# One transfer for a segment's rows, one buffer for the sums of q and k

## The chip, the cores and the metric

The kernel runs on one core of one Trainium2 chip. The metric is the time of one execution on the device, in microseconds; of several executions the median is taken. The core has five engines that matter here: PE (TensorE: matmuls, and PEld, its weight loads), DVE (VectorE), ACT (ScalarE), POOL (GpSimd) and SP (SyncE, which here only issues transfers). Sixteen DMA engines move the data. ACT and POOL issue transfers as well.

## What is computed

Two independent blocks are added to x. The first is attention with a recurrent memory: x is cut into 64 segments of 32 rows; each segment's attention sees 8 memory rows and its own 32, and the memory for the next segment is the attention's output at the memory rows. So segment s + 1 cannot begin before segment s is through its output projection. The second block normalizes two routed rows (C = 2) and sends them through a gated feed-forward network of width 3584; it runs at the end and is not touched by the change.

```python
def _A_ref(x, mem0, Wq, Wk, Wv, Wo, seg_len):   # x normalized, D = 1024, H = 32, E = 128, M = 8, seg_len = 32
    mem = mem0
    for s in range(n_seg):                      # 64
        xs = x[:, s * seg_len:(s + 1) * seg_len, :].copy()
        h = jnp.concatenate([mem, xs], axis=1)
        q = jnp.einsum('btd,dhe->bhte', h, Wq)
        k = jnp.einsum('btd,dhe->bhte', h, Wk)
        v = jnp.einsum('btd,dhe->bhte', h, Wv)
        scores = jnp.einsum('bhqe,bhke->bhqk', q, k) * scale
        scores = jnp.where(mask[None, None], scores, -1000000000.0)
        p = _softmax(scores, axis=-1)
        o = jnp.einsum('bhqk,bhke->bhqe', p, v)
        o = jnp.einsum('bhte,hed->btd', o, Wo)
        mem = o[:, :M, :].copy()
        outs.append(o[:, M:, :])
...
    return x + _A_ref(xn, A_mem0, A_Wq, A_Wk, A_Wv, A_Wo, A_seg_len) + _B_ref(xn, B_w_r, B_w_gate, B_w_up, B_w_down)
```

## The kernel before

**Weights.** The four matrices are cut into 64 granules of 512 KB, `g` = 0 to 63: 8 for each of the six phases q0, k0, q1, k1, v0, v1 (matrix and half of the heads, `PHASES`), and 16 for the output projection (`w` = 0 to 15). 44 granules stay in SBUF; 20 are streamed in every segment through a pool of five slots (`g`, `N_SLOT`). Of these, granule 10 is put together from copies kept in PSUM and needs no transfer (`kept_piece`), granule 19 is fetched by half. SP issues a fetch (`fetch`, L317) each time a streamed granule has been used, so the fetches run up to four granules ahead of PE. In the first segment the streamed granules are also copied to a scratch in DRAM (`wsc`), from which all later ones come.

**Rows.** A segment's 32 rows by 1024 columns lie in `XN` as 128 partitions by 256: four blocks of 256 columns (`g` in the row patterns, not a granule), each 32 partitions high. In each block the first 24 partitions (`XM`) hold the segment's first 24 rows, the other 8 the memory's. The segment's last 8 rows (the left rows) of four segments are taken together, one pass for a group `G` of four segments; `j` = s mod 4 is the place in the group. So the passes `left_pass` fall on different phases: v with j = 0, q of the next group with j = 1, k with j = 2, the left rows' output with j = 3 (`WL`). Their q and k sums go out to DRAM (`ql_d`, by `store_ql`, L656) and come back per segment as `LX` (L450), which `turn_lx` transposes at place (1, 5).

**Order.** Everything is emitted by hand. Within a segment a place is (phase, granule of the phase); `hook` puts a function behind that granule's matmuls. At the end of a phase for q or k ACT copies the sum out of PSUM into `XB` (L653); at (p + 1, 3) PE turns it (`transposes`) and it becomes `QT` or `KT`. `scores` stands at (2, 6) and (4, 6), `soften` (the softmax: exponent on ACT, then sums and products on DVE into `PT2`) at (3, 0) and (5, 0), `attend` at (5, 4), (5, 6) and in the projection. `load_seg` for the next segment is issued by POOL at (2, 0), `norm_seg` uses its rows at the segment's end. The result `WO` is copied by ACT and DVE into `OB`, which is `XN` (L752, L753), stored by POOL (L755), and turned into the next segment's memory rows. With j = 3 the left rows' result is stored a segment later, `store_left` at (2, 4), from a buffer tagged vl, which the same segment's `VL` then takes at the end of phase 4.

**Buffers.** The pool `one` has one buffer for each tag; a tile waits until all uses of the tile before it under the same tag are done. Tags that matter: bE is taken by XB of q, QT, the second PT2, and with j = 2 by XBl (the left rows' sum of k, second half, which waits there for its store to `ql_d`); kt by XB of k, KT and the first half of OT; bA by LX, the first XBl with j = 2, the first PT2, one half of VM.

**Transfers and semaphores.** Each transfer signals one of eight semaphores in turn, one ring of eight for those that SP and ACT issue, one for POOL's. An issue waits until the transfer eight places before it in its ring has landed.

Of the kernel before, what the change touches and what calls it, by code (L numbers as in the profile page):

```python
# [8 lines left out]
BF16 = mybir.dt.bfloat16  # L9
# [3 lines left out]
ACTF = mybir.ActivationFunctionType  # L13
# [15 lines left out]
def kernel(  # L29
# [16 lines left out]
    nc = tc.nc  # L46
    P = 128
# [3 lines left out]
    SEG = int(A_seg_len)  # L51
# [8 lines left out]
    SCALE = float(E) ** -0.5  # L60
    XM = SEG - M
# [3 lines left out]
    x2 = A_x[0]  # L65
    out2 = out[0]
# [27 lines left out]
    one = ctx.enter_context(tc.tile_pool(name="one", bufs=1, reuse_waits="tile"))  # L94
# [34 lines left out]
    XN = const.tile([P, 256], BF16, name="XN")  # L129
# [10 lines left out]
    SPS = BS[:, 0:8 * NK].rearrange("p (i a k) -> p i a k", i=4, a=2)  # L140
# [33 lines left out]
    for s in range(4):  # L174
        nc.vector.tensor_copy(out=SELM[:, s, :, 0:XM],
                              in_=IDENT[:, 32 * s:32 * s + XM].unsqueeze(1).to_broadcast([P, 4, XM]))
        nc.vector.tensor_copy(out=SELL[:, s, :, :],
                              in_=IDENT.rearrange("p (s c) -> p s c", c=32)[:, :, XM:SEG])
# [67 lines left out]
        return t  # L246

    def load_seg(s):
        for g in range(4):
            nc.gpsimd.dma_start(out=XN[32 * g:32 * g + XM, :], in_=x2[s * SEG:s * SEG + XM, 256 * g:256 * (g + 1)])  # L250

    def norm_seg(s):
        mr = two_rows(MR[:, s, :], "ri")
# [238 lines left out]
    for s in range(NSEG):  # L492
        G, j = divmod(s, 4)
# [7 lines left out]
        def hook(p, kc, fn):  # L501
            hooks.setdefault((p, kc), []).append(fn)
# [16 lines left out]
        def scores(half):  # L519
            QKL = qkl[0]  # L520
            q, k = QT[half], KT[half]
            for il in range(4):
                for jq in range(4):
                    hh = 4 * il + jq
                    nc.tensor.matmul(SPS[32 * jq:32 * jq + 32, il, 0, :], lhsT=q[:, hh, :], rhs=k[:, hh, :],
                                     start=(il == 0), stop=True, tile_position=(0, 32 * jq), skip_group_check=True)
                    nc.tensor.matmul(SPS[32 * jq:32 * jq + XL, il, 1, :], lhsT=QKL[:, il, 2 * half, jq, :],  # L527
                                     rhs=k[:, hh, :], start=False, stop=True, tile_position=(0, 32 * jq),
                                     skip_group_check=True)
            for S4, m in ((SPS[:, :, 0, 0:XM], MASK), (SPS[:, :, 0, SEG:NK], None),  # L530
                          (SPS[:, :, 1, SEG:NK], MASK[:, 0:XL])):
                if m is not None:
                    m = m.unsqueeze(1).to_broadcast([P, 4, S4.shape[2]])
                    nc.vector.tensor_tensor(out=S4, in0=S4, in1=m, op=ALU.add)  # L534
                else:
                    nc.vector.tensor_scalar(out=S4, in0=S4, scalar1=NEGR, scalar2=None, op0=ALU.add)
            S8 = SPS.rearrange("p i a k -> p (i a) k")
            NM = one.tile([P, 8], F32, tag="nm", name="NM")
            nc.vector.tensor_reduce(out=NM[:, :], in_=S8, axis=AX.X, op=ALU.max, negate=True)  # L539
            nc.vector.tensor_tensor(out=S8, in0=S8, in1=NM[:, :].unsqueeze(2).to_broadcast([P, 8, NK]), op=ALU.add)  # L540

        def soften(half):
            S8 = SPS.rearrange("p i a k -> p (i a) k")
            nc.scalar.activation(out=S8, in_=S8, func=ACTF.Exp, scale=SCALE)  # L544
            DN = one.tile([P, 8], F32, tag="nm", name="DN")
            nc.vector.tensor_reduce(out=DN[:, :], in_=S8, axis=AX.X, op=ALU.add)
            nc.vector.reciprocal(out=DN[:, :], in_=DN[:, :])
            PT2 = one.tile([P, 2, 4, 64], BF16, tag=("bA", "bE")[half], name="PT2")
            PTm, PTl = PT2[:, 0], PT2[:, 1]
            PM = PTl.rearrange("p i q -> p (i q)").rearrange("p (b k) -> p b k", b=8)  # L550
            PLt = PL.rearrange("p i a k -> p (i a) k")
            dnb = DN[:, :].unsqueeze(2)
            nc.vector.tensor_tensor(out=PM, in0=S8[:, :, 0:32], in1=dnb.to_broadcast([P, 8, 32]), op=ALU.mult)
            nc.vector.tensor_tensor(out=PLt[:, :, XL * j:XL * (j + 1)], in0=S8[:, :, 32:NK],
                                    in1=dnb.to_broadcast([P, 8, XL]), op=ALU.mult)
            nc.vector.transpose(out=PTm.rearrange("p i q -> p (i q)"), in_=PM.rearrange("p b k -> p (b k)"))
            nc.vector.transpose(out=PTl.rearrange("p i q -> p (i q)"), in_=PLt.rearrange("p b k -> p (b k)"))
            PTs[half] = (PTm, PTl)
# [45 lines left out]
            hook(1, 2, lambda: kept_piece(KEPT_PART, 3, nc.vector.tensor_copy))  # L604
            hook(1, 5, turn_lx)
        hook(2, 6, lambda: scores(0))
        hook(3, 0, lambda: soften(0))
        if s + 1 < NSEG:
            hook(2, 0, lambda: load_seg(s + 1))
        if j == 3 or (j == 0 and G + 1 < NT):  # L610
            hook(2 if j else 3, 0, get_left)
            hook(5, 3, prep_left)
        hook(4, 6, lambda: scores(1))
        hook(5, 0, lambda: soften(1))
        hook(5, 4, lambda: attend(0, 0))
        hook(5, 6, lambda: attend(0, 1))
# [7 lines left out]
        for p, (mat, half) in enumerate(PHASES):  # L624
            PSm = psA.tile([P, 512], F32, tag="acc", name="PSm")
            PSl, done = None, []
            if mat in left:
                PSl, done = started.pop((s, p), (None, []))
                if PSl is None:
                    PSl = psL.tile([P, 512], F32, tag="accl", name="PSl")  # L630
            rest = [8 * p + kc for kc in range(KC) if 8 * p + kc not in done]
            behind = []
            for kc in range(KC):
                g = 8 * p + kc
                Gv = granule(g)
                for jq in range(4):
                    nc.tensor.matmul(PSm[32 * jq:32 * jq + 32, :], lhsT=ST[:, kc, :], rhs=part(Gv, jq),  # L637
                                     start=(kc == 0), stop=(kc == KC - 1), tile_position=(0, 32 * jq))
                if g in KEPT_COLS and s == 0:
                    keep(g, Gv)  # L640
                behind.append((g, Gv))
                if PSl is None or kc >= 3 or not left_before:
                    for g_, Gv_ in behind:
                        if PSl is not None and g_ not in done:
                            left_pass(PSl, g_, Gv_, not done and g_ == rest[0], g_ == rest[-1])
                        after(s, g_)
                    behind = []
                for fn in hooks.pop((p, kc), []):
                    fn()
            left_before = PSl is not None  # L650
            if mat < 2:
                XB = one.tile([P, 512], BF16, tag=("bE", "kt")[mat], name="XB")
                nc.scalar.copy(out=XB[:, :], in_=PSm[:, :])  # L653
                hooks.setdefault((p + 1, 3), []).insert(0, lambda m=mat, h=half, b=XB: transposes(m, h, b))

                def store_ql(mat=mat, half=half, PSl=PSl):  # L656
                    if mat == 0:
                        XBl = left_out()[:, 2:4].rearrange("p s r h -> p (s r h)")
                    else:
                        XBl = one.tile([P, 512], BF16, tag=("bA", "vl" if s == 0 else "bE")[half], name="XBl")[:, :]  # L660
                    nc.scalar.copy(out=XBl, in_=PSl[:, :])
                    if s == 0:
                        hooks[p + 1, 3].insert(0, lambda m=mat, h=half, b=XBl: turn_first(m, h, b))
                    nc.scalar.dma_start(out=ql_d[left[mat]][2 * half + mat], in_=XBl)


                if PSl is not None and s == 0:
                    store_ql()
                elif PSl is not None and mat == 1 and half == 1:
                    nxt["ql"] = store_ql  # L670
                elif PSl is not None:
                    hooks.setdefault((p + 1, 0), []).append(store_ql)
            else:
                c0 = half * 512
                VM[half] = one.tile([P, 512], BF16, tag=("bC", "bA")[half], name="VM")
                nc.scalar.copy(out=VM[half][:, :], in_=PSm[:, :])  # L676
                if PSl is not None:
                    if half == 0:
                        group["vl"] = one.tile([P, 1024], BF16, tag="vl", name="VL")
                    nc.scalar.copy(out=group["vl"][:, c0:c0 + 512], in_=PSl[:, :])  # L680
# [70 lines left out]
        OB = XN  # L751
        nc.scalar.copy(out=OB[:, 0:P], in_=WO[:, 0:P])  # L752
        nc.vector.tensor_copy(out=OB[:, P:256], in_=WO[:, P:256])  # L753
        for g in range(4):
            nc.gpsimd.dma_start(out=out2[s * SEG:s * SEG + XM, 256 * g:256 * (g + 1)], in_=OB[32 * g:32 * g + XM, :])  # L755
        n1 = (len(fill) + 1) // 2
        for fn in fill[:n1]:
            fn()
# [119 lines left out]
```

## Time and profile before

| | us |
|---|---|
| three runs | 2021.12, 2021.41, 2036.9 |
| median | 2021.41 |
| the profiled execution | 2031.99 |
| its span, first to last instruction | 2030.4 |
| PE / PEld busy | 1648.3 / 887.1 |
| DVE / ACT / POOL busy | 889.5 / 734.6 / 435.0 |
| granted TensorE clock, mean | 0.952 |

A profile shows one execution. Its page has the busy time of each engine, the span in 40 slices (a digit is the busy share in tenths), the DMA queues with packets, MB and share of sixteen engines' span, the chain of work that ended last, the costliest groups of instructions and the DMA issues. In a row of a group, the first bar is followed by busy time and mean duration in ns, the second by the idle time of the engine ahead of these instructions and by what ended it. In the timeline a bracket holds the idle time ahead of an instruction and its releaser. q1 is SP's queue, q10 ACT's, q0 POOL's; q8 and q14 load instructions. A busy PE is not PE at its peak, since matmuls overlap.

### The profile page before, as it was taken

Reading aid. Unit: us, or ns where it says so; the run is one execution under the profiler, and the core shown is the slowest. Engines: PE = TensorE matmul, PEld = TensorE weight load, DVE = VectorE, ACT = ScalarE, POOL = GpSimd, SP = SyncE. Lnnn points to the kernel's source line nnn. Section 1 sums busy time; section 2 is a strip of 40 time slices with the busy share of each in tenths; the row PEclk is TensorE's granted clock in tenths of the full one; section 3 lists DMA queues with packets and bytes.
Section 4 is the critical chain, followed back from the end, with each engine's and each line's share of the span. In section 5 each row is a group of like instructions: output and inputs, shape, how many; then the busy total and the mean of one; then the engine's idle time right before and its main releaser. Section 6 shows DMA issues by size and latency. Waiting matters only on the chain.

```text
span 2030.4 us, 82766 instructions
## 1 busy us (share of the span) xinstructions
PE 1648.3 (81%) x36024; PEld 887.1 (44%) x36024; DVE 889.5 (44%) x2845; ACT 734.6 (36%) x1995; POOL 435.0 (21%) x881
## 2 busy tenths in 40 slices
PE   3468887889888888888889898888878887988855
PEld 1124444445444444444444444545444443545433
DVE  4834434444443444434444444445444444444420
ACT  0123343433333333333434344333434333343320
POOL 3021211222221211222131122222131212212120
PEclk8669998999999999999999999999999999999986
DMA  9989999999989999999999999999999999999996
GB/s 366 372 301 362 337 359 328 341 369 346 362 322 367 347 351 360 340 350 328 362 360 349 369 365 375 342 357 350 373 354 345 364 344 354 347 362 339 375 381 260
DMA packets 232557, 712.43 MB, mean 351 GB/s; under 512 B 39361, under 2 KB 53729, under 8 KB 232193
## 3 DMA queue, kind: packets, MB, share of 16 engines
q1 hardware_dynamic: 194368, 671.17, 89.4%
q0 software_dynamic: 28608, 27.57, 4.4%
q10 hardware_dynamic: 9216, 8.39, 1.2%
q8 instruction: 282, 4.62, 0.9%
q14 instruction: 83, 0.67, 0.1%
HBM read 694.32 MB, written 22.29 MB: 353 GB/s over the span
## 4 chain that ended last, share of the span: by engine, by line
DMA 45%; PE 33%; DVE 8%; ACT 6%; issue 6%; POOL 1%; ACTq 0%; SPq 0%; DVEq 0%; POOLq 0%
DMA g<-wsc 30%; PE PSm L637 12%; DMA ql_d<-XBl 8%; PE WO L692 7%; PE PSl L620 4%; PE BT L507 2%; DMA out_dram<-OL 2%; PE WL L692 2%; ACT OTL L581 1%; DVE BS L540 1%; DVE NM L539 1%; DVE BS L534 1%; ACT XB L653 1%; ACT QT L512 1%; PE BS L572 1%
## 5 line engine op out<-in xcount | busy, mean ns | idle before, releaser
L637 PE MATMUL PSm<-wres,ST 128*32 128x512 bf16 x8448 | 713.6, 390 | 15.5 <-issue 5.6
L637 PEld LDWEIGHTS <-ST 128*32 128x32 bf16 x12288 | 323.7, 97 | 479.3 <-issue 221.1
L637 PE MATMUL PSm<-g,ST 128*32 128x512 bf16 x3840 | 393.0, 392 | 145.3 <-DMA g<-wsc 122.8
L653 ACT CAST XB<-PSm 128x512 bf16<-128x512 f32 x256 | 150.2, 587 | 362.0 <-PE PSm L637 306.9
L692 PE MATMUL WO<-wres,OT 128*32 128x256 bf16 x5632 | 231.9, 278 | 17.5 <-DMA wres<-in_A_Wo_dram 10.2
L450 POOL DMA_DIRECT2D LX<-ql_d x63 | 33.6, 534 | 981.6 <-DVE OTL L581 509.5
L692 PEld LDWEIGHTS <-OT 128*32 128x32 bf16 x8192 | 199.5, 97 | 94.7 <-issue 75.9
L517 DVE COPY KT<-BT 128x512 bf16<-128x512 bf16 x128 | 53.7, 419 | 421.9 <-PE BT L507 413.4
L620 PE MATMUL PSl<-wres,STL 128*32 128x512 bf16 x2112 | 200.7, 391 | 9.1 <-ACT VL L680 7.0
L250 POOL DMA_DIRECT2D XN<-in_A_x_dram x256 | 129.0, 508 | 220.4 <-PE PSm L637 72.8
L755 POOL DMA_DIRECT2D out_dram<-XN x256 | 129.3, 513 | 205.3 <-DVE XN L753 202.4
L692 PE MATMUL WO<-g,OT 128*32 128x256 bf16 x2560 | 132.6, 282 | 19.4 <-DMA g<-wsc 10.4
L346 DVE COPY g<-KEPT 128x512 bf16<-128x512 bf16 x252 | 95.2, 419 | 88.6 <-PE PSm L637 55.3
L507 PE MATMUL BT<-IDENT,XB 128*128 128x128 bf16 x1024 | 102.9, 224 | 24.8 <-ACT XB L653 19.3
L507 PEld LDWEIGHTS <-XB 128*128 128x128 bf16 x1024 | 59.0, 98 | 132.0 <-ACT XB L653 82.0
L676 ACT CAST VM<-PSm 128x512 bf16<-128x512 f32 x128 | 79.8, 624 | 95.0 <-PE PSm L637 95.0
L620 PEld LDWEIGHTS <-STL 128*32 128x32 bf16 x3072 | 83.0, 98 | 69.8 <-issue 23.4
L534 DVE TENSOR_TENSOR BS<-BS,CT 128x96 f32<-128x96 f32 (+1 forms) x256 | 59.7, 233 | 103.8 <-PE BS L527 99.4
L572 PEld LDWEIGHTS <-VM 32*128 32x128 bf16 x2048 | 69.4, 91 | 77.5 <-issue 67.7
L544 ACT ACTIVATE BS<-BS 128x320 f32<-128x320 f32 x128 | 54.0, 422 | 131.9 <-DVE BS L540 131.9
L620 PE MATMUL PSl<-g,STL 128*32 128x512 bf16 x960 | 98.1, 393 | 0.8 <-issue 0.7
L753 DVE CAST XN<-WO 128x128 bf16<-128x128 f32 x64 | 18.7, 292 | 179.5 <-ACT XN L752 179.5
(156 smaller groups left out, 2396.6 us busy)
## 6 DMA issues: line engine op xcount, KB each, us to landing
g<-wsc SPq DMA_DIRECT2D x1134, 512.0 KB, 5.9
g<-wsc SPq DMA_DIRECT2D x63, 256.0 KB, 4.9
LX<-ql_d POOLq DMA_DIRECT2D x63, 128.0 KB, 6.3
MW<-in_B_w_gate_dram SPq DMA_DIRECT2D x16, 448.0 KB, 9.4
MW<-in_B_w_up_dram SPq DMA_DIRECT2D x16, 448.0 KB, 9.1
wres<-in_A_Wk_dram SPq DMA_DIRECT2D x12, 512.0 KB, 13.6
MW<-in_B_w_down_dram SPq DMA_DIRECT2D x12, 512.0 KB, 10.3
wres<-in_A_Wv_dram SPq DMA_DIRECT2D x11, 512.0 KB, 9.7
```

The lines of the kernel that those rows point to most:

```text
L250: nc.gpsimd.dma_start(out=XN[32 * g:32 * g + XM, :], in_=x2[s * SEG:s * SEG + XM, 256 * g:256 * (g + 1)])
L346: copy(out=t[:, 512 * c:512 * (c + 1)], in_=KEPT_COLS[g][c])
L507: nc.tensor.transpose(out=PTq[:, il, :, :].rearrange("p j r -> p (j r)"), in_=XB[:, il * P:(il + 1) * P], identity=IDENT[:, :])
L534: nc.vector.tensor_tensor(out=S4, in0=S4, in1=m, op=ALU.add)
L544: nc.scalar.activation(out=S8, in_=S8, func=ACTF.Exp, scale=SCALE)
L572: nc.tensor.matmul(o, lhsT=VM[half][q0:q0 + 32, il * P:(il + 1) * P], rhs=PTm[q0:q0 + 32, il, 0:NK], start=True, stop=False, tile_position ...
L620: nc.tensor.matmul(PSl[32 * jq:32 * jq + 32, :], lhsT=STL[:, g % KC, :], rhs=part(Gv, jq), start=first_, stop=last_, tile_position=(0, 32 ...
L637: nc.tensor.matmul(PSm[32 * jq:32 * jq + 32, :], lhsT=ST[:, kc, :], rhs=part(Gv, jq), start=(kc == 0), stop=(kc == KC - 1), tile_position= ...
L653: nc.scalar.copy(out=XB[:, :], in_=PSm[:, :])
L676: nc.scalar.copy(out=VM[half][:, :], in_=PSm[:, :])
L692: nc.tensor.matmul(PS[32 * g:32 * g + 32, 0:256], lhsT=lhs(h), rhs=Gv[:, D * hs + 256 * g:D * hs + 256 * (g + 1)], start=False, stop=(last ...
L755: nc.gpsimd.dma_start(out=out2[s * SEG:s * SEG + XM, 256 * g:256 * (g + 1)], in_=OB[32 * g:32 * g + XM, :])
```

## The change

1. `XB` of q takes the tag kt as XB of k does, in place of bE.
2. `load_seg` issues one transfer on POOL for all 32 rows of the segment, four blocks of 32 partitions by 256 columns, in place of four transfers of 24 rows. The 8 partitions of each block that were left alone get the segment's left rows, which `norm_seg` masks.
3. The store of the result is one transfer, issued by ACT in place of four by POOL. It writes 32 rows; the last 8, the memory's, are written over when `store_left` stores the group.
4. `soften` is split: the exponent (`exponent`) stays at (3, 0) and (5, 0); the rest of the first half moves from (3, 0) to (3, 4) with j = 2 and in segment 0. The second half stays at (5, 0).

```diff
     def load_seg(s):
-        for g in range(4):
-            nc.gpsimd.dma_start(out=XN[32 * g:32 * g + XM, :], in_=x2[s * SEG:s * SEG + XM, 256 * g:256 * (g + 1)])
+        nc.gpsimd.dma_start(out=XN[:, :], in_=x2[s * SEG:(s + 1) * SEG, :].rearrange("r (g c) -> g r c", g=4))
...
+        def exponent():
+            S8 = SPS.rearrange("p i a k -> p (i a) k")
+            nc.scalar.activation(out=S8, in_=S8, func=ACTF.Exp, scale=SCALE)
+
         def soften(half):
             S8 = SPS.rearrange("p i a k -> p (i a) k")
-            nc.scalar.activation(out=S8, in_=S8, func=ACTF.Exp, scale=SCALE)
             DN = one.tile([P, 8], F32, tag="nm", name="DN")
...
         hook(2, 6, lambda: scores(0))
-        hook(3, 0, lambda: soften(0))
+        hook(3, 0, exponent)
+        hook(3, 4 if j == 2 or s == 0 else 0, lambda: soften(0))
...
         hook(4, 6, lambda: scores(1))
+        hook(5, 0, exponent)
         hook(5, 0, lambda: soften(1))
...
             if mat < 2:
-                XB = one.tile([P, 512], BF16, tag=("bE", "kt")[mat], name="XB")
+                XB = one.tile([P, 512], BF16, tag="kt", name="XB")
...
         nc.vector.tensor_copy(out=OB[:, P:256], in_=WO[:, P:256])
-        for g in range(4):
-            nc.gpsimd.dma_start(out=out2[s * SEG:s * SEG + XM, 256 * g:256 * (g + 1)], in_=OB[32 * g:32 * g + XM, :])
+
+        nc.scalar.dma_start(out=out2[s * SEG:(s + 1) * SEG, :].rearrange("r (g c) -> g r c", g=4), in_=OB[:, :])
```

## The prediction

> **What bounds the kernel now.** I read the page first (span, the DMA slices, the queues, the chain that ended last), then windows over four neighbouring segments, then the table of waits, the table of DMA issues and a few pieces of the timeline.
>
> ```profile
> span 2030.4 us, 82766 instructions
> DMA  9989999999989999999999999999999999999996
> DMA packets 232557, 712.43 MB, mean 351 GB/s; under 512 B 39361, under 2 KB 53729, under 8 KB 232193
> q1 hardware_dynamic: 194368, 671.17, 89.4%
> q10 hardware_dynamic: 9216, 8.39, 1.2%
> DMA 45%; PE 33%; DVE 8%; ACT 6%; issue 6%; POOL 1%; ACTq 0%; SPq 0%; DVEq 0%; POOLq 0%
> ```
>
> The DMA engines are busy nine tenths or more in nearly every slice, and 45% of the chain that ended last is DMA. The profiled execution took 2031.99 us in all (1.6 around its span); the three timed runs are 2021.12, 2021.41 and 2036.9, so it lies inside their spread. I add my sum to it and carry the same difference to the median.
>
> A segment here runs from the end of ACT's copy of the result (L752) to the next such end. The windows give stretch, length, busy time of PE, PEld, DVE, ACT and POOL, granted clock, DMA share, GB/s. The first four are segments with j = 0, 1, 2, 3; then come the first six microseconds of the j = 1 segment and nine from its middle.
>
> ```profile
> 349.08:380.31 31.23, 26.47 (x625) 14.97 (x615) 13.09 (x43) 12.02 (x34) 9.49 (x18) 1.00 0.91 315
> 380.31:409.10 28.79, 24.37 (x533) 12.89 (x530) 12.51 (x40) 11.45 (x33) 4.75 (x10) 1.00 0.98 371
> 409.10:436.86 27.76, 24.45 (x537) 12.94 (x536) 12.39 (x40) 11.41 (x32) 4.70 (x10) 1.00 0.97 359
> 436.86:464.43 27.57, 23.41 (x536) 13.10 (x538) 13.38 (x45) 10.50 (x31) 7.05 (x14) 1.00 1.01 373
> 380.31:386.31 6.00, 4.71 (x78) 2.11 (x74) 1.99 (x6) 1.74 (x5) 2.37 (x6) 1.00 0.97 359
> 394.31:403.31 9.00, 7.27 (x177) 3.60 (x173) 6.60 (x23) 5.17 (x16) 0.00 (x0) 1.00 1.03 407
> ```
>
> With j = 1, 2, 3 the weight stream fills the DMA engines (0.97 to 1.01); with j = 0 there is some 9% of room. PE is close behind, so a saving on PE alone is soon eaten by a wait for the stream, while DMA work added in three of four segments has little to hide in.
>
> ```profile
> PE PSm L637 <- DMA g<-wsc: 122.8, 200, 2.3
> ACT XB L653 <- DMA ql_d<-XBl: 55.0, 11, 6.7
> PE BT L507 <- ACT XB L653: 19.3, 28, 2.5
> DVE PT L553 <- DMA ql_d<-XBl: 38.5, 15, 3.6
> L620 PE MATMUL PSl<-wres,STL 128*32 128x512 bf16 x2112 | 200.7, 391 | 9.1 <-ACT VL L680 7.0 <-issue 0.4
> ```
>
> **The sums in the keys' buffer.** After a j = 2 segment XBl lies in buffer bE until its store has read it, and the next segment's first XB waits for that: 55.0 us on ACT. PE feels only part, at the transposes in place (1, 3): at most 19.3 us, other segments' included. One case in full, ACT and then PE, j = 3:
>
> ```profile
> 324.84 0.59 ACT L653 CAST XB<-PSm 128x512 bf16<-128x512 f32 x1 [6.67 <-DMA ql_d<-XBl]
> 325.48 0.61 PE L507 MATMUL BT<-IDENT,XB 128*128 128x128 bf16 x4 [2.46 <-ACT XB L653]
> ```
>
> In kt, XB waits only for matmuls of the segment before, half a projection back on PE. But QT stays in bE, so the wait moves to QT, one copy (0.59) and four transposes (0.61) later; PE meets it two granules on, where LX is turned through the same PSUM bank. So at most some 1.2 us of a case is gained: 0 to 13 us over 11 cases. As the stream is the next limit in just these segments I take -3.
>
> **The later softmax.** In the built program the order on PE and DVE with j = 2 is unchanged: nothing stands on DVE between the old place and the new one. So the 38.5 us of PT waiting stay: 0. In segment 0 six DVE instructions move behind four router tiles on a DVE without gaps: 0.
>
> **The transfers.** First, how transfers were dealt to DMA engines before (table of issues; KB each, median us to landing):
>
> ```profile
> g<-wsc SPq DMA_DIRECT2D x1134, 512.0 KB, 5.9
> MISC<-in_B_w_r_dram SPq DMA_DIRECT2D x1, 256.0 KB, 5.2
> LX<-ql_d POOLq DMA_DIRECT2D x63, 128.0 KB, 6.3
> XN<-in_A_x_dram POOLq DMA_DIRECT2D x256, 12.0 KB, 5.2
> ql_d<-OTL ACTq DMA_DIRECT2D x32, 128.0 KB, 5.7
> ql_d<-XBl ACTq DMA_DIRECT2D x32, 128.0 KB, 7.2
> out_dram<-XN POOLq DMA_DIRECT2D x256, 12.0 KB, 4.8
> wsc<-in_A_Wq_dram POOLq DMA_DIRECT2D x5, 512.0 KB, 10.3
> wsc<-in_A_Wq_dram POOLq DMA_DIRECT2D x1, 256.0 KB, 10.6
> XL<-in_A_x_dram POOLq DMA_DIRECT2D x128, 16.0 KB, 5.5
> out_dram<-OL POOLq DMA_DIRECT2D x64, 16.0 KB, 5.7
> MEM<-in_A_mem_dram POOLq DMA_DIRECT2D x4, 4.0 KB, 4.7
> ```
>
> ACT's 64 ql_d stores make 9216 packets: 144 each, 128 rows of 1 KB plus sixteen small ones. Packets of 512 B to 2 KB number 53729 - 39361 = 14368; less 8192 of ql_d and 32 rows of MEM, 6144 are left for the 512 XN loads and stores: twelve each, two rows a packet. So 24 rows went to twelve engines; packed to 4 KB they would be three packets. SP issued 1316 transfers (16 rows, first and last shown), so q1 has 194368 - 16 x 1316 = 173312 data packets; of 178464 packets between 2 and 8 KB, 5152 are POOL's. The wsc copies (19 in five rows, first and last shown) make 2368 at 4 KB, the 63 LX 2016; 768 are left for 192 XL and OL transfers: exactly four each. Their rows stand in the access pattern as 4 x 8. The new load and store stand there as 4 x 32, four blocks of 256 columns. So I expect each on four of the sixteen engines, 32 rows an engine.
>
> The Trainium skill (DMA: Bandwidth & Descriptors, "Why a DMA increments its semaphore by 16 and not by 1") gives the number of engines as the largest up to 16 that divides the slowest dimension of both patterns, and for ACT's queue the lowest-numbered ones, every time the same. The trace agrees with twelve and four; which engines they are no run here shows.
>
> Price of the store: q10 took 1.2% of 2030.4 us on 16 engines, 24.4 us an engine for 576 packets: 42 ns, 48 without the small ones. A row of 512 B costs between half and all of that, 21 to 48; I take 35 from the middle, so 32 x 35 = 1.12 us on four engines (0.67 to 1.54). Taken away are 6144 packets x 45 ns / 16 / 64 = 0.27 us per segment and engine. Net +0.85 (0.40 to 1.27), plus 4 x 168 ns = 0.67 where the load (four 4 KB packets an engine; 89.4% x 2030.4 / 10832 = 168 ns) meets the same four. A granule is there when its slowest engine is done. With j = 0 the 9% of room hides this; in the other 47 segments I let half through, as they have stretches under full share: 0.85 x 0.5 x 47 = **+20** (0 to 1.94 x 47 = 91).
>
> Who waits for the store: its sixteen-engine relatives land after 5.7 to 7.2 us with eight packets an engine. If the 24 further packets take turns with the stream's, they add 24 x (168 + 35) ns = 4.9: landing 10.6 to 12.1 after issue; without turns 6.5. The Trainium skill (same page, "Queues, rings and completion order") says that an engine goes round its queues packet by packet.
>
> SP's transfers and the store now share a ring of eight semaphores, so in the built program the eighth such transfer behind the store waits until it has landed: with j = 1 and 2 SP's seventh fetch of the segment, with j = 0 and 3 the eighth. SP in a j = 1 and a j = 2 segment, and POOL's old store, then the late case in the same j = 0 segment:
>
> ```profile
> 383.01 7.79 SPq L326 DMA_DIRECT2D g<-wsc  x7
> 411.06 6.08 SPq L326 DMA_DIRECT2D g<-wsc  x6
> 417.69 0.32 SPq L326 DMA_DIRECT2D g<-wsc  x1
> 349.69 2.04 POOL L755 DMA_DIRECT2D out_dram<-XN  x4 [2.66 <-DVE XN L753]
> 361.11 0.51 POOL L250 DMA_DIRECT2D XN<-in_A_x_dram  x1 [2.93 <-issue]
> 361.69 2.41 POOL L769 DMA_DIRECT2D out_dram<-OL  x4
> 369.63 0.59 ACT L680 CAST VL<-PSl 128x512 bf16<-128x512 f32 x1 [1.86 <-DMA out_dram<-OL]
> ```
>
> The store can go 0.6 us into the segment (349.69 against 349.08), so it lands at +11.2 to 12.7. The seventh fetch stood at +8.6 (j = 2) and +10.2 (j = 1, the last of the seven): held 2.6 to 4.1 and 1.0 to 2.5 us, with all later fetches queued behind it. Three fetches in flight give the engines 3 x 8 x 168 ns = 4 us of cover; for the thinner queue behind it I take 0.7 us with j = 2: **+11** (0 to 6.6 x 16 = 106).
>
> On POOL the next load waits for the landing too, and with j = 0 the four OL stores stand behind it, and VL behind them. In the segment shown the last load went at +12.0, OL from +12.6, and VL came 1.86 us late; PE lost 7.0 us to this in all. Now OL would start at +11.8 to 13.3 in all fifteen: 1 us each, less the 7.0: **+8** (-7 if none is late; 15 x 1.86 - 7 = +21 if all are as late as this one).
>
> ACT's own cost, one issue more behind DVE's copy, lies in its idle stretch before XB (6.67 us in the case above). POOL's seven fewer issues per segment were off the path, since POOL works 4.70 of 27.76 us.
>
> Sum: -3 + 20 + 11 + 8 = +36: the profiled execution 2068, the median 2057.
>
> **The rivals.**
>
> *All sixteen engines.* If the pattern is dealt evenly, or the store's small packets slip in beside the stream's, store and load cost what they cost before and the store lands like ql_d, before +8.6. XB's gain remains: 2021 - 4 = 2017. Against it: the exact fours.
>
> *Fewer transfers free the seam (faster).* At the start of a segment the engines move 359 GB/s at full share, in the middle 407. If the eight small transfers cause that, their going gives 12% of 6 us, 0.7 us in each of 63 segments: 2021 - 44 = 1977. It decides if the small transfers hold the stream up by more than their own packets. Against it: LX and ql_d lie in the same stretch and stay. The Trainium skill (same page, Bandwidth, "Measured") calls transfers under 64 KB dominated by descriptors, which speaks for this rival; no row here separates it.
>
> *SP's hold passes whole.* If the store lands past +12.7, the cover is used up: 3.4 x 16 + 1.7 x 16 = 82 in place of 11: 2128.
>
> **How the numbers follow.** Forecast 0.60, its own range 2030 to 2100; sixteen engines 0.20; free seam 0.12; SP's hold 0.08. The range 2010 to 2100 takes the first two and leaves out the last two. One per cent is 20 us, a little over the spread of the runs shown. Slower by more: the forecast but its lowest part (0.53) and SP's hold: 0.61. Within: 0.20 + 0.07 = 0.27. Faster: 0.12.
>
> **What would show it.** q10 grows by 8192 packets plus small ones, and packets of 512 B to 2 KB change by +2048 if the load goes in 4 KB packets (6144 go, 8192 come). The store's landing median over 10 us, POOL's XN waiting on it, SP waiting on out_dram<-XN, and more than 122.8 us of PE waiting on g would bear the forecast out. ACT's XB should no longer wait for ql_d, QT should. A store that lands in 6 to 7 us makes the forecast wrong, as does a four-engine store with PE's wait on g unchanged.

## The result and the profile after

| | before | after |
|---|---|---|
| median of 20 runs each, us | 2030.12 (2011.28 to 2041.23) | 2046.25 (2032.45 to 2066.22) |
| the profiled execution, us | 2031.99 | 2043.11 |
| its span, us | 2030.4 | 2041.6 |
| PE / PEld busy, us | 1648.3 / 887.1 | 1655.9 / 891.4 |
| DVE / ACT / POOL busy, us | 889.5 / 734.6 / 435.0 | 889.7 / 740.7 / 218.0 |
| granted clock | 0.952 | 0.948 |

The changed kernel takes 1.008 times as long, 95% interval [1.0058, 1.0102]. That is some 16 us on 2030, inside the band of one per cent that the prediction called "within", to which it gave 0.27; it gave 0.61 to a larger loss. The forecast was +36.

First the page of the changed kernel: span, DMA slices and packets, the queues, the chain that ended last.

```profile
span 2041.6 us, 82132 instructions
DMA  9989999999999999999999999999999999999996
DMA packets 229735, 714.53 MB, mean 350 GB/s; under 512 B 33472, under 2 KB 49888, under 8 KB 229376
q1 hardware_dynamic: 194368, 671.17, 89.4%
q10 hardware_dynamic: 17664, 12.59, 1.9%
DMA 49%; PE 34%; DVE 7%; issue 5%; ACT 4%; SPq 0%; ACTq 0%; POOL 0%; POOLq 0%; DVEq 0%
```

q10 grew by 17664 - 9216 = 8448 packets, 64 times 132: 128 rows of 512 B and four small packets for each store, where a ql_d store has sixteen. So the store runs on four engines. Packets of 512 B to 2 KB went from 14368 to 49888 - 33472 = 16416, the +2048 that was expected if the load goes in 4-KB packets: sixteen a load. That these lie on four engines, four on each, is read from POOL's packets of 8 and 32 B, counted in the traces: four for each transfer on twelve engines, none for a load on sixteen (e6 below), 48 for each single load. That is one for every packet that an engine without a share goes without, 12 x 4 here. The DMA share of the chain rose from 45% to 49%.

Next the table of waits of the changed kernel (who waited for whom, us in total, times, longest), then the DMA queue's own waits of SP, then the windows over the same four neighbouring segments, j = 0 to 3.

```profile
PE PSm L641 <- DMA g<-wsc: 157.0, 251, 1.8
POOL XN L249 <- DMA out_dram<-XN: 86.2, 11, 13.5
DVE PT L555 <- DMA ql_d<-XBl: 41.0, 15, 3.8
POOL out_dram L773 <- DMA out_dram<-XN: 38.4, 1, 38.4
ACT QT L511 <- DMA ql_d<-XBl: 7.5, 5, 1.9
PE BT L506 <- ACT XB L657: 2.1, 5, 1.0
PE PSl L624 <- ACT VL L684: 1.5, 3, 0.8
```

```profile
SPq L325 <- DMA g<-wsc: 419.9, 562, 3.8
SPq L369 <- DMA out_dram<-XN: 7.2, 1, 7.2
```

```profile
345.86:378.42 32.56, 27.59 (x627) 15.30 (x615) 13.08 (x43) 12.32 (x34) 6.02 (x11) 0.95 0.89 310
378.42:406.84 28.42, 24.38 (x541) 12.79 (x537) 12.42 (x40) 11.62 (x31) 1.37 (x3) 1.00 0.98 355
406.84:436.12 29.28, 24.13 (x533) 12.35 (x529) 12.40 (x40) 11.50 (x32) 1.37 (x3) 1.00 0.99 355
436.12:464.91 28.79, 23.57 (x534) 12.84 (x538) 13.46 (x45) 10.61 (x29) 3.67 (x7) 1.00 0.99 364
```

What to read here: PE's wait for the stream went from 122.8 to 157.0 us. XB no longer waits for ql_d, QT does a little (7.5), and PE's wait for XB fell from 19.3 to 2.1. PT's wait is what it was. VL is no later than before, it is earlier (7.0 to 1.5). SP waits for the store once, in line 369, which is the feed-forward part at the end. POOL's busy time in a segment with j = 1 or 2 fell from 4.7 to 1.37 us.

The four segments shown are 3.7 us longer in sum than the same four before, but single segments scatter. From the fourth segment on, the mean segment with j = 0, 1, 2, 3 takes 29.96, 28.43, 27.69, 29.34 us before and 29.75, 28.51, 27.78, 29.86 now (worked out from the two traces). So a group of four loses half a microsecond, with j = 3, and the segments with j = 1 and 2 are no shorter for POOL's shorter work.

One place off the segments is new. Between the end of ACT's last copy of the result and the end of the span lie 2041.56 - 1967.81 = 73.75 us, and 2030.44 - 1960.48 = 69.96 before. The chain that ended last shows that stretch, of the changed kernel and then of the kernel before (start, us, what):

```profile
1967.84 0.30 DVE XN L757
1968.14 0.02 issue
1968.16 8.10 DMA out_dram<-XN
...
1977.01 1.75 POOL out_dram L773 x3
1978.76 6.17 DMA out_dram<-OL
```

```profile
1962.92 1.81 PE WL L692 x57
1964.74 0.02 issue
1964.76 0.38 ACT OL L766
1965.14 0.28 issue
1965.42 1.82 POOL out_dram L769 x3
1967.24 5.54 DMA out_dram<-OL
```

The single store writes the memory's rows too, where the last eight rows of the group belong; so the last store of the left rows has to wait until the result's store has landed (8.10 us). It starts 9.2 us behind the copy (1977.01 - 1967.81) in place of 4.9 (1965.42 - 1960.48), and the routed rows are read behind it. Of these 4.3 us, 3.8 are left at the end of the span. The four profiles with the single store on ACT (after, e3, e5, e12) have 72.6 to 74.2 us in this stretch, the ten others 68.1 to 71.8; as e4, whose store holds the left rows back too, has 70.65, the size is known to a microsecond or two. Before the last segment the left rows are stored a segment later and don't meet it. So of the profile's 11.1 us, 7.3 lie in the segments and 3.8 behind them.

### The profile page after: what moved, and what is told of

It reads as the page before. It is cut to its first block, busy times and chain, and to the rows that moved or that the text cites. A ratio compares the mean times of both kernels' runs of the same rounds, so it can differ in the third digit from the quotient of the medians.

```text
span 2041.6 us, 82132 instructions
## 1 busy us (share of the span) xinstructions
PE 1655.9 (81%) x36024; PEld 891.4 (44%) x36024; DVE 889.7 (44%) x2845; ACT 740.7 (36%) x1995; POOL 218.0 (11%) x433
## 2 busy tenths in 40 slices
DMA packets 229735, 714.53 MB, mean 350 GB/s; under 512 B 33472, under 2 KB 49888, under 8 KB 229376
## 3 DMA queue, kind: packets, MB, share of 16 engines
q10 hardware_dynamic: 17664, 12.59, 1.9%
## 4 chain that ended last, share of the span: by engine, by line
DMA 49%; PE 34%; DVE 7%; issue 5%; ACT 4%; SPq 0%; ACTq 0%; POOL 0%; POOLq 0%; DVEq 0%
DMA g<-wsc 39%; PE PSm L641 13%; PE WO L696 8%; DMA ql_d<-XBl 5%; PE PSl L624 4%; PE WL L696 2%; PE BT L506 1%; ACT OTL L583 1%; PE BS L574 1%; DMA g<-in_A_Wk_dram 1%; DVE XR L225 1%; DMA XP<-in_A_x_dram 1%; DMA wres<-in_A_Wo_dram 1%; PE BT L456 1%; DVE BS L539 1%
## 5 line engine op out<-in xcount | busy, mean ns | idle before, releaser
L641 PE MATMUL PSm<-wres,ST 128*32 128x512 bf16 x8448 | 708.6, 388 | 11.2 <-DVE ST L279 5.4
L641 PE MATMUL PSm<-g,ST 128*32 128x512 bf16 x3840 | 389.9, 390 | 179.0 <-DMA g<-wsc 157.0
L696 PE MATMUL WO<-wres,OT 128*32 128x256 bf16 x5632 | 236.1, 283 | 17.4 <-DMA wres<-in_A_Wo_dram 10.2
L511 ACT COPY QT<-BT 128x512 bf16<-128x512 bf16 x128 | 75.1, 587 | 69.3 <-PE BT L506 55.5
L249 POOL DMA_DIRECT2D XN<-in_A_x_dram x64 | 43.8, 685 | 512.3 <-PE PSm L641 166.6
## 6 DMA issues: line engine op xcount, KB each, us to landing
wres<-in_A_Wk_dram SPq DMA_DIRECT2D x12, 512.0 KB, 11.2
```

Of the source, the lines that this page charges most:

```text
L511: nc.scalar.copy(out=QT[half][:, :, :], in_=pv)
L696: nc.tensor.matmul(PS[32 * g:32 * g + 32, 0:256], lhsT=lhs(h), rhs=Gv[:, D * hs + 256 * g:D * hs + 256 * (g + 1)], start=False, stop=(last ...
```

## The experiments

Twelve runs were made, in three groups (e1 to e4, e5 to e8, e9 to e12), each group on another chip; each ratio is against the kernel before on the same chip, with a 95% interval. A profile shows one execution of a run, and its waits need not be the run's typical ones.

**e1: XB alone**

```diff
-                XB = one.tile([P, 512], BF16, tag=("bE", "kt")[mat], name="XB")
+                XB = one.tile([P, 512], BF16, tag="kt", name="XB")
```

> The kernel before with one edit: XB of q takes the tag kt. Every theory expects a small gain, since XB's 55.0 us of waiting for ql_d goes from ACT but QT stays in bE and takes the wait over: ratio to the kernel before 0.994 to 1.000 (-13 to 0 us), likeliest 0.9985 (-3 us). In the trace ACT's XB should have no ql_d row; ACT's QT or PE's scores should have one. If it comes out at 0.99 or below, the wait was worth far more than PE's 19.3 us of idle time showed, and the rest of the change cost more than 1%.

Measured 1.0004 [0.9971, 1.0036]. The waits of e1 beside those of before: XB's row for ql_d is gone, QT takes over 3.9 us, PE waits 13.6 us less for XB, and 20.6 us more for the stream.

```profile
ACT QT L512 <- DMA ql_d<-XBl: 3.9, 3, 1.8
PE BT L507 <- ACT XB L653: 5.7, 12, 1.0
PE PSm L637 <- DMA g<-wsc: 143.4, 217, 2.7
```

With j = 3 the first XB copy starts 4.90 us into the segment in place of 5.73, the mean over the trace, but the segment is shorter by only 0.26 us (29.08 against 29.34): the rest is handed to the stream a few granules on.

**e2 and e9: the load alone** (the same kernel twice)

```diff
-        for g in range(4):
-            nc.gpsimd.dma_start(out=XN[32 * g:32 * g + XM, :], in_=x2[s * SEG:s * SEG + XM, 256 * g:256 * (g + 1)])
+        nc.gpsimd.dma_start(out=XN[:, :], in_=x2[s * SEG:(s + 1) * SEG, :].rearrange("r (g c) -> g r c", g=4))
```

> The kernel before with one edit: load_seg is one transfer of 32 rows (four engines, four 4-KB packets each) in place of four of 24 rows. Theory A (what costs is that four of the sixteen engines carry more than the others): 16 x 168 ns = 0.67 us more on four engines in each of 64 segments, half let through with j = 1 to 3: 1.004 to 1.008. Theory B (what costs is SP's wait in the shared ring of semaphores): nothing, 0.998 to 1.002, as POOL's ring is its own. Theory C (fewer small transfers help the stream): 0.990 to 0.998.

> The kernel of e2 once more (before, with the single load alone), beside the next two in the same call. e2 gave 1.0129 [1.0085, 1.0173], while the changed kernel with the old stores, which has the single load too, gave 1.0047 [1.0017, 1.0078]; one of XB, the softmax or e2's six runs has to explain that. If XB and the softmax are worth nothing, as the prediction had it, this comes out nearer to 1.007 than to 1.013. If they are worth 0.8% together, it stays at 1.010 or above.

Measured 1.0129 [1.0085, 1.0173] and 1.0086 [1.005, 1.0122]; weighted by their intervals 1.0103, about 21 us: a little above theory A's band (e9's interval reaches into it), and above B's and C's. e2's page, waits and DMA issues:

```profile
DMA packets 229481, 713.52 MB, mean 348 GB/s; under 512 B 38336, under 2 KB 49632, under 8 KB 229120
```

```profile
PE PSm L636 <- DMA g<-wsc: 163.7, 233, 2.9
```

```profile
XN<-in_A_x_dram POOLq DMA_DIRECT2D x64, 64.0 KB, 6.6
```

The class of 2 to 8 KB grew from 178464 to 229120 - 49632 = 179488, by 1024 = 64 x 16, so the load's form is the one in the changed kernel. PE's wait for the stream is 40.9 us longer than before (28.6 in e9). The load, one part of four, costs more than the whole change.

**e3: the store alone** (before, with the changed kernel's store)

```diff
-        for g in range(4):
-            nc.gpsimd.dma_start(out=out2[s * SEG:s * SEG + XM, 256 * g:256 * (g + 1)], in_=OB[32 * g:32 * g + XM, :])
+        nc.scalar.dma_start(out=out2[s * SEG:(s + 1) * SEG, :].rearrange("r (g c) -> g r c", g=4), in_=OB[:, :])
```

> The kernel before with one edit: the store of the result is one transfer on ACT of 32 rows (four engines) in place of four on POOL of 24 rows. Theory A: the store's part of the four engines' load, 32 packets of 512 B, is 32 x 27 to 35 ns = 0.9 to 1.1 us a segment: 1.005 to 1.010. Theory B: all of the change's loss stands here, 1.008 to 1.011, with SP shown waiting for out_dram<-XN or fetches that go later. Theory C: 0.990 to 0.998. Should e1 be 0.9985 and e2 1.000, the sum of the parts must give the changed kernel's 1.008, so that this one is 1.009.

Measured 1.0042 [1.0009, 1.0074], a little under A's band (from 1.005), further under B's (from 1.008), with an interval that reaches into A's. PE's wait for the stream is 134.4, 11.6 us above that of before, and SP waits for the store once, at the end:

```profile
PE PSm L637 <- DMA g<-wsc: 134.4, 211, 2.1
```

```profile
SPq L370 <- DMA out_dram<-XN: 5.8, 1, 5.8
```

**e4: the single store on POOL** (changed kernel, `nc.gpsimd.dma_start` for `nc.scalar.dma_start` in the store)

> The changed kernel with one edit: the same single store is issued by POOL in place of ACT. It stays on four engines, and it leaves the ring of semaphores that SP's fetches use. Against the kernel before: theory A expects what the changed kernel has, 1.006 to 1.010; theory B expects that the loss goes, 0.996 to 1.002 (XB's gain and the load remain). If POOL's queue deals it otherwise (0 small packets on q10, and the packets of 512 B gone from q0 as 4-KB ones), theory A would gain too, and the packet table must be read first.

Measured 1.0152 [1.0112, 1.0191]: slower than with the store on ACT, so taking the store out of SP's ring gains nothing. It is above theory A's band too (1.006 to 1.010). POOL deals the rows otherwise than ACT: its queue has 1024 more packets of 4 KB than in the changed kernel, sixteen a store, and the 512-B packets on q10 are gone. The store's landing is on the page here:

```profile
out_dram<-XN POOLq DMA_DIRECT2D x64, 64.0 KB, 5.5
```

**e5: the single load on ACT** (changed kernel, `nc.scalar.dma_start` for `nc.gpsimd.dma_start` in `load_seg`)

> The changed kernel with one edit: the load of a segment's rows is issued by ACT in place of POOL, still one transfer on four engines, so that load and store share ACT's queue. The load alone gave 1.013, the store alone 1.004, both together 1.008. Theory A (any share that falls on four engines holds the stream up by what it adds there): load and store now add up on one set of four, 16 to 20 us more than the changed kernel if its two sets differ, and the same if they do not: 1.008 to 1.018. Theory D (ACT's queue always takes the same four engines, and those are ahead of the others; POOL's takes another four each time and so meets the last engine in some segments): 0.998 to 1.004, below the changed kernel. Theory E (POOL's single load costs by what POOL's queue adds to it, 48 packets of 32 B a load): 1.002 to 1.005, which is the store's part alone.

Measured 1.012 [1.0088, 1.0152]. Taken by the time alone this would bear out theory A and strike D and E. The waits say otherwise: SP's own, then the others of e5.

```profile
SPq L325 <- DMA XN<-in_A_x_dram: 60.0, 24, 5.2
```

```profile
PE PSm L641 <- DMA g<-wsc: 140.3, 234, 2.3
DVE PT L555 <- DMA ql_d<-XBl: 50.6, 15, 5.4
PE BS L524 <- DVE KT L516: 22.6, 13, 3.5
```

PE's wait for the stream fell by 16.7 us against the changed kernel, but SP is held behind the load 24 times, PT's buffer comes free later (41.0 to 50.6), and the scores wait longer for KT (22.6; 8.1 in the changed kernel, 9.8 to 18.2 in the others). The load also goes later with j = 3 (9.2 us into the segment in place of 7.7), and as packets of 512 B in place of 4 KB. The run put other costs in the load's place; it does not tell A from D and E.

**e6: the load on sixteen engines** (before, with the load's 24 rows, `XM`, made 32 in all four transfers)

> The kernel before with one edit: load_seg is four transfers on POOL of 32 rows in place of 24, so that sixteen engines take two rows each (64 KB in all, as in the single load, but no engine gets more than eight packets of 512 B or four of 1 KB). Theories A and D (the loss is in the dealing): 0.998 to 1.003. If the loss is in the rows themselves (a third more bytes, 33% more to read from x): 1.009 to 1.015. The packet table should show 64 x 4 x 16 packets of 1 KB and no dummy packets on idle engines.

Measured 1.0023 [0.9995, 1.0052]: 5 us, from -1 to +11. The added 16 KB a segment are 1.05 MB in all, 3 us at the 351 GB/s of before. PE's wait for the stream is no longer than the 122.8 us of before, though this profile's execution took 2025.87 us, under the run's median of 2036.47.

```profile
PE PSm L637 <- DMA g<-wsc: 116.2, 193, 2.9
```

The same 64 KB a segment cost little when four transfers deal them to sixteen engines. So neither the rows nor the bytes are the most of what the single load pays for.

**e7: the store on sixteen engines** (changed kernel)

```diff
-        nc.scalar.dma_start(out=out2[s * SEG:(s + 1) * SEG, :].rearrange("r (g c) -> g r c", g=4), in_=OB[:, :])
+        for g in range(4):
+            nc.scalar.dma_start(out=out2[s * SEG:(s + 1) * SEG, 256 * g:256 * (g + 1)], in_=OB[32 * g:32 * (g + 1), :])
```

> The changed kernel with one edit: the store is four transfers on ACT, one per block of 32 partitions, each on sixteen engines, in place of one on four. Theory A: the store's share of the loss goes and the load's stays: 1.004 to 1.013, not above the changed kernel's 1.008 by more than the interval if sets of four coincide. Theory B (SP's ring): four places of the ring in place of one, so SP's fetches would wait for the stores more often: 1.010 to 1.02. Theory D: the store was hidden on engines that were ahead, and dealing it to all brings it back on the last one: 1.008 to 1.015.

Measured 1.0337 [1.0299, 1.0375], 52 us above the changed kernel and past every band. SP's own waits:

```profile
SPq L325 <- DMA ql_d<-XBl: 66.2, 10, 8.1
SPq L325 <- DMA out_dram<-XN: 54.5, 27, 7.5
```

This is SP's hold, with four places of the ring in place of one: fetches wait for the stores and, as the ring comes round sooner, for the slow ql_d stores. With j = 3 the mean segment takes 32.08 us against 29.86 in the changed kernel, some two thirds of the 52 us over sixteen segments, and in its third phase PE waits 2.27 us for the stream where it waited 0.08.

**e8 and e11: the single load with XB in kt.** e8 is the changed kernel with the four old stores, e11 the kernel before with the load of e2 and XB of e1. They differ by the softmax move alone.

> The changed kernel with one edit: the store of before, four transfers on POOL of 24 rows. It keeps the single load, XB in kt and the later softmax. If the parts add up, and XB and the softmax are worth nothing: 1.010 to 1.016, as the single load alone. If it comes out at 1.004 or below, XB and the softmax together are worth what the sum of the parts lacks (1.013 + 0.004 against 1.008), and the store on ACT costs its 0.004. If it comes out at 1.010 or above, the store on ACT gains where the load is single, which theory A does not give and theory D only if the load then moves off the late engines.

> The kernel before with the single load and XB of q in kt, without the softmax move and with the old stores. If XB gives nothing whatever the stream does: the same as e9. If XB's earlier copy is worth more when the stream is later: 1.003 to 1.006, at the value of the changed kernel with the old stores, and e9 above 1.009. If it is the softmax: the same as e9, both at 1.009 or above.

Measured 1.0047 [1.0017, 1.0078] and 1.0097 [1.0064, 1.0131], weighted 1.0070. e11 is no faster than the load alone (1.0103), so no gain of XB is seen beside the single load; e8, with the softmax move, is 0.005 below e11.

**e10: XB and the softmax without the transfers** (changed kernel, old load and old store)

> The changed kernel with load and store of before: what is left of the change is XB of q in kt and the later softmax. By the prediction's terms (-3 and 0 us): 0.997 to 1.001, as XB alone gave 1.0004 [0.9971, 1.0036]. If the later softmax is what makes up the sum of the parts: 0.990 to 0.993, and this kernel is the best of all. In the trace PT's wait for ql_d should stand near 38.5 us if the move does nothing.

Measured 0.9955 [0.9928, 0.9983], the fastest of all, and faster than both kernels. PT's wait did not move (38.5 before):

```profile
DVE PT L556 <- DMA ql_d<-XBl: 40.0, 15, 3.7
PE PSm L642 <- DMA g<-wsc: 143.2, 222, 2.8
```

What the softmax has to do with it is open. In the built programs e10 and e1 have the same instructions with the same waits in the same order, but for one place: in segment 0 six DVE instructions of the softmax stand behind four router tiles. The first segment's end lies 0.5 us earlier in e10's profile (140.85 against 141.37), and 1.0 us earlier in e8's than in e11's (140.07 against 141.08); yet the ratios of both pairs differ by 0.005. Nothing in the profiles holds the other 9 us; but e10's profiled execution took 2034.06 us, at a median of 2020.68, so it can't show a gain.

Two readings are left. If the twins are one kernel each, XB (with or without the softmax) has 0.9976, 5 us, and the distance between twins tells how far an interval of 0.3% can be trusted. If the ratios stand as measured, XB gives nothing and the softmax move 10 us: the two pairs together lie 0.005 apart with an interval of 0.003, which chance alone hardly gives. The twins of each pair ran on different chips, and no run has both on one. The sums below take the first reading, and say where the second differs.

**e12: the changed kernel with the load of e6**

> The changed kernel with one edit: the load is four transfers on POOL of 32 rows, on sixteen engines each, in place of one on four; the single store on ACT stays. Theory A: the load's share of the loss (0.007 to 0.013) goes and the store's 0.004 stays: 0.997 to 1.004. If the store takes over what the load leaves (the last engine is then the store's): 1.005 to 1.010, no gain against the changed kernel.

Measured 0.9988 [0.9954, 1.0021]. One edit, the dealing of the load, takes back the whole loss: 1.008 - 0.9988 = 0.009, some 19 us. It goes from one transfer on four engines to four on sixteen; no run has one transfer on sixteen, so what the dealing does isn't parted from what the single issue does.

**Where the single load costs.** For each kernel, the wait of PE for streamed granules in two phases, k1 and v0, which follow the load (the single load on POOL is issued 5.5 to 7.9 us into the segment and lands some 6.5 later): mean of each j over the segments from the fourth on, the four j added up; worked out from each trace.

```
us per four segments      k1 + v0
single load on POOL:   after 4.60, e2 4.94, e9 4.60, e11 4.45, e8 4.98, e4 4.89, e7 3.85
four loads on POOL:    before 2.82, e1 3.54, e10 3.46, e3 3.53, e6 2.90, e12 3.41
single load on ACT:    e5 3.17
```

Without e7, whose time is lost a phase earlier, six kernels with the single load on POOL lie at 4.45 to 4.98, and all seven others at 2.82 to 3.54. The means are 4.74 and 3.26; 1.48 us a group of four over 63 segments is 23 us, the 21 that the times give. In the first two phases, before the load, the same sum is 3.74 before, 4.14 in e1, and 4.20 and 3.88 in e2 and e9: no such parting. Over all six phases the parting stands: 9.58 to 10.42 for the six, 7.40 to 9.17 for the seven. In length the load's loss lies with j = 2 and 3: the mean segments are longer than before by 0.51 and 1.09 us in e2 and by 0.66 and 0.64 in e9, and no longer with j = 0 and 1.

## Why the prediction was partly right

**The forecast's direction and the range held; of +36 us, 16 came.** By the runs' ratios on 2030 us: the load +21, XB with the softmax -5, the store between +2 (1.008 less the 1.0070 of e8 and e11) and +9 (e3), 3.8 of which the chain shows at the end. The sum is 18 to 25, each part uncertain by some 5, against 16 measured. By the second reading of the twins the store is +7 (1.008 less the 1.0047 of e8) and XB with the softmax -9 (e10): 19 in sum, which fits as well. Of the prediction's four terms (-3, +20, +11, +8) the second had its size for another part of the change, the third came to nothing and the fourth turned over. That the sum fell into the range is partly luck.

**The sums in the keys' buffer: right in the mechanism, the size not told from nothing.** -3 was said; e1 alone gives 0 (-6 to +7), the twins taken as one -5. The 55.0 us of ACT's wait went, PE kept what was named (XB's row 19.3 to 5.7 in e1), and the stream took it back (20.6 us more), as argued.

**The later softmax: right on the order and on PT's row** (38.5, 41.0 in the changed kernel), open in the time: 0 was said, and both pairs of twins have half a per cent for it, without a cause that the profiles show.

**Four engines: right in its premise, and in size by accident.** The exact fours were borne out by four small packets on q10 for each store. But the +20 was the store's: "Net +0.85 (0.40 to 1.27), plus 4 x 168 ns = 0.67 where the load meets the same four". The load went into the upper end only. The runs turn it round: the load alone is +21, and the store in the segments at most a few us. The step that failed is that term's split; the load's net on its own four engines, 0.67 less half the 0.27 that was taken away for both, let through by half, would have been 0.53 x 0.5 x 47 = 13, two thirds of what was measured. Nor is it 47 segments: with j = 1 the load alone costs nothing that shows, and with j = 2 and 3 it costs 0.5 to 1.1 us each.

**Why the store is cheaper than the load is not settled.** It isn't the place in the segment: e4 issues the store at the same place on POOL (0.6 us into the segment; 0.4 on ACT) and has 0.8% more than e8 and e11 together, 1.05% more than e8, from which it differs in the store alone: about what the load costs. It seems not to be the load as such: on ACT (e5) the wait after it is gone, though the time is not. So, as far as these runs go, a share of four engines costs when POOL issues it, and less when ACT does; for the load on ACT that rests on the waits alone. Three readings fit. The Trainium skill (DMA: Bandwidth & Descriptors, "Why a DMA increments its semaphore by 16 and not by 1") has ACT's queue take the lowest-numbered engines each time and POOL's go on from a cursor, so the store would always lie on the same four, which may be ahead of the last one, and the load would come round to the late ones; no run here shows which engine a packet was on. Or it is the form: POOL's share is four packets of 4 KB an engine, ACT's 32 of 512 B. Or it is what POOL's queue adds, the 48 packets of 32 B of theory E; in the changed kernel's trace they take 15 ns each, 0.06 us for four on an engine, so their own time is too short for it. None of the three was tried by itself.

**SP's hold: the mechanism is real, its size here nothing.** +11 rested on the store landing 10.6 to 12.1 us behind its issue. The page has no landing for it, but POOL's next load waits for it, and eleven times it was the last to come. Timeline of one such case, ACT and then POOL, in a segment that begins at 1213.75:

```profile
1213.48 0.27 ACT L756 CAST XN<-WO 128x128 bf16<-128x128 f32 x1 [2.49 <-PE WO L696]
1214.10 0.55 ACTq L759 DMA_DIRECT2D out_dram<-XN  x1
```

```profile
1217.76 0.68 POOL L249 DMA_DIRECT2D XN<-in_A_x_dram  x1 [6.86 <-DMA out_dram<-XN]
```

Here the load could go 3.7 us after the store's issue, over the eleven cases 3.2 to 6.0, so the store had landed by then. The packets tell of all 64 stores: of a store's 128 the first starts 2.7 us and the last 4.8 us behind the issue, in the mean, and the last of any store 8.1. The wrong step is the turns: "If the 24 further packets take turns with the stream's, they add 24 x (168 + 35) ns". In the trace the 512-B packets take 27 ns each (35 was assumed). In turns with the stream's packets an engine's 32 would need 32 x (27 + 168) ns = 6.2 us; from a store's first packet to its last it is 2.1 in the mean and 5.0 at the most. So they pass faster than in turns one by one, though 32 without a break would need only 0.9. The rule that was cited for turns (the Trainium skill, same page, "Queues, rings and completion order") speaks of a packet of some 9 to 17 descriptors, at most 64, and I read it as one packet of the profile's list. A whole share of 32 rows could be one or a few packets of the rule; read so, the trace doesn't speak against it, but no run shows where a packet of the rule ends. So the seventh fetch, 8.6 us and later in the segment, never met the store: SP's table has no wait of a streamed fetch for it. e7 shows what it is when it does: 54.5 and 66.2 us on SP, 52 us of time.

**POOL and VL: wrong in sign.** +8 (-7 to +21) was put on OL and VL for the same late landing. In the changed kernel OL is issued 11.2 us into the segment in place of 11.7 (the mean of its four stores), as POOL has one load to issue ahead of it and not four, and PE's wait for VL fell from 7.0 to 1.5. The 7.0 is the longest of all fourteen profiles; e1, e6 and e10, which have four loads and the old store as well, have 3.1 to 4.4. So it is a gain of some 2 to 5 us, near the low end.

**Not seen at all: the end.** The store's eight extra rows cost 3.8 us once, behind the last segment. The change's text had it ("the last 8 are written over"), and the prediction asked who waits for the store in every segment, but not in the last, where the left rows' store follows at once.

**The rivals.** "All sixteen engines" falls by the four small packets. "Fewer transfers free the seam" falls by e2 and e9: three transfers fewer at each load, and 1% slower where the rival needed a gain. The Trainium skill's warning that transfers under 64 KB are dominated by descriptors (same page, Bandwidth) would favour the single one; here the four small ones on twelve or sixteen engines win (1.000 and 1.0023 against 1.0103). "SP's hold passes whole" needs a store past 12.7 us into the segment; the last packet of any store started 8.1 us behind the issue.

## What to carry over

Beside a stream that fills the DMA engines, fewer transfers is no gain by itself: look at how the pattern deals a transfer to the engines. Here four transfers on twelve or sixteen engines were worth keeping against one on four. Ask of every issue moved to a queue that shares a ring of semaphores how many places it takes (one held SP up once, at the end; four cost 2.6%), and of every store that writes more than it must who has to write there next, in the last pass above all. And measure each part alone: this change was a gain of some 0.2 to 0.5% and a loss of 1% put together, and with the load dealt to sixteen engines (e12), or without the transfers (e10), it is as fast as the kernel before or up to 0.5% faster.

## What the runs showed that was not expected

Under a stream that fills the engines, a store of 128 rows of 512 B on four engines starts its last packet 4.8 us after its issue in the mean (8.1 at the latest), about when each of the four 12-KB transfers on twelve engines lands (4.8 by the page before). The same 64 KB on four engines cost 0.8 to 1% when POOL issued them (e2, e9 and e4) and 0.1 to 0.4% as ACT's store. And two programs alike but for one place in the first segment came out 0.5% apart in two pairs (e1 and e10, e11 and e8), with intervals that overlap only at their ends; the cause is open.
